# The first rows of a token mixer: statistics behind low parts, products by readiness, shorter scales

## The chip, the cores and the metric

The kernel runs on one core of a Trainium2 chip. The metric is device time in microseconds (us) of that core, the median of several runs. The engines work at the same time and wait for each other on semaphores: TensorE (PE in the profile) for matrix products, VectorE (DVE), ScalarE (ACT), GpSimd (POOL), and SyncE (SP), which here only issues loads and stores. Each engine works through its own queue in order.

## What is computed

```python
xn = layernorm(x)                                    # x: (1, 2048, 512), over the last axis
s  = irfft2(rfft2(xn) * (w_r + 1j * w_i))            # spectral branch
u  = gelu(einsum("bsd,sf->bdf", layernorm(xn), w1) + b1)   # w1: (2048, 1792)
y  = einsum("bdf,fs->bds", u, w2) + b2               # w2: (1792, 2048)
out = x + s * silu(y.transpose(0, 2, 1))
```

The layer norm is applied twice in the token branch and once in the spectral branch, so every token needs two factors: `rs[0]` and `rs[1]`, one over the root of `v2[0]` = var + eps and of `v2[1]` = var (1 + eps) + eps squared. The token branch uses `rs[1]` alone; the spectral branch takes the product `q` of `rs[0]`, `rs[1]` and `v2[1]`.

## The kernel before

Tokens are split into 16 rows of 128 partitions x 512 channels. Every operand of the big products is split into a high part (rounded) and a low part (the rest), and a product is made as high x high, high x low and low x high. In the first stage, 16 turns `j` of a loop accumulate six blocks of the hidden layer (two halves `a` of three blocks, `NE1`), in banks 0 to 5. This stage starts while the loads still run; the change touches its first rows. Later stages (the other hidden blocks, the spectral filter, the second weight product) are not touched.

**One row.** For row `j`, VectorE takes the statistics of x (`stats`, `bn_stats`), `spreads` turns them into mean and variance and into `v2`, ScalarE takes the square root (`sd`), and `scales` makes the factors on VectorE: the reciprocal `r0`, one Newton step (`t` = `r0`², `t` times -0.5 times `v2`, `rs` = (1.5 + `t`) times `r0`), then `nb`, minus mean times `rs[1]`; GpSimd multiplies `q`. ScalarE makes `h` from x by `nb` and `rs[1]` (`normed`, two halves) and its high part `hh` by a rounding copy (`high`), VectorE the low part `hl` (`low`). The weights of the row come as two raw tiles, `raws[j, 0]` and `raws[j, 1]`; ScalarE rounds each to its high part (`w1h`) and VectorE makes its low part (`w1l`), which the trace calls `w1l<-w1r,w1h`. `turned` makes the row's factor table `cf` from `q` on ScalarE, for the small transform of the spectral branch, which every second turn puts between the products.

**Row 0** is made differently: VectorE writes `hh[0]` straight from x (`normed_v`), between the factors and `nb`.

**Products.** `hidden_early` gives per half `a`: three products high x high, three with the low weights, then (after the transform where there is one) three with the low h. That makes six groups of three per row.

**Order.** All these instructions are kept in the order of the program on each engine (`keep`), so the order of the code is the order of each engine's queue. Turn 0 is special (`early` is false): it also takes the statistics of rows 2 and 3, before the low parts of row 1. From turn 1 on, turn `j` takes the statistics of row `j + 3` before the low parts of row `j + 1`; at even turns `spreads` and `scales` handle two rows at a time.

**Loads.** x comes in pairs of rows (`load_x`, three buffers), weights in pairs of rows (`w1_load`, two buffers per half), each as two DMAs. For row 0, row 1's x and weights, the DMAs are issued one by one by SP, ScalarE and GpSimd (`issued`). A load into a used buffer waits until its readers are done.

Before the first row, TensorE multiplies zeros (tile `wz`) 18 times.

Of the kernel before, what the change touches and what calls it, by code (L numbers as in the profile page):

```python
# [16 lines left out]
P = 128  # L17
# [125 lines left out]
def spectral_mixer_kernel(tc, x, w1, b1, w2, b2, wk, we, wx, c_f, c_ft, c_d, c_i, c_g, c_h, c_t, out):  # L143
# [19 lines left out]
    with tc.tile_pool(name="ps", bufs=1, space=PSUM) as psp, ExitStack() as left, ExitStack() as right:  # L163
# [54 lines left out]

        def stats(m, i, src):
            keep(V.bn_stats(m["st"][:, i], src))  # L220
# [12 lines left out]
        def scales(m, between=lambda: None):  # L233
# [6 lines left out]

            G.tensor_mul(m["q"], m["rs"][:, :, 0:1], m["rs"][:, :, 1:2])
            G.tensor_mul(m["q"], m["q"], m["v2"][:, :, 1:2])
# [206 lines left out]

        def hidden_early(j, nf, bank, w, between):  # L450
            def products(wi, hj, first, last):
                for i in range(nf):
                    T.matmul(ps[:, bank + i], w[wi][:, i * P:(i + 1) * P], hj, start=first and j == 0, stop=last and j == NJ - 1)
            products(0, hh[j], True, False)
            products(1, hh[j], False, False)
            r = between()
            products(0, hl[j], False, True)
            return r

        stats(m, 0, xs[0])  # L460
        spreads(m, 1)
# [3 lines left out]
        scales(m, lambda: normed_v(hh[0], xs[0], m, 0, 1))  # L465
# [4 lines left out]
        high(w[1][0], raws[0, 1])  # L470
        spreads(m1, 1)
        low(hl[0], h, hh[0])
        scales(m1)
        low(w[1][1], raws[0, 1], w[1][0])
        of = {0: (m, 0), 1: (m1, 0)}
# [8 lines left out]
        for j in range(NJ):  # L484
# [16 lines left out]
            hidden_early(j, NE1, 0, w[0], first_transform if j % 2 or j == NJ - 2 else lambda: None)  # L501
            hidden_early(j, NE1, NE1, w[1], lambda: None)

            early = j > 0
            if more:
                w = w1_tiles(j + 1)
                h = new_h(j + 1)
                if not early:
                    high(w[0][0], raws[j + 1, 0])
                normed(h, xs[j + 1], *of[j + 1])  # L510
                high(hh[j + 1], h)
                if early and j + 3 < NJ:
                    stats(of[j + 3][0], of[j + 3][1], xs[j + 3])
                    if j % 2 == 0:
                        spreads(of[j + 2][0], 2)
# [5 lines left out]
            if more:  # L521
                if early and j % 2 == 0 and j + 2 < NJ:
                    scales(of[j + 2][0])
                if not early:
# [3 lines left out]
                low(w[0][1], raws[j + 1, 0], w[0][0])  # L528
                high(w[1][0], raws[j + 1, 1])
                low(hl[j + 1], h, hh[j + 1])  # L530
                for i in range(j + early, j + 2):
                    turns[i] = turned(i, *of[i])
            run(folds)
            if more:
# [6 lines left out]
                if not early:  # L541
                    scales(m)
                if j % 2 == 0 and j + 4 < NJ:
# [560 lines left out]
```

## Time and profile before

| | us |
|---|---|
| median of 3 runs | 369.25 |
| lowest, highest | 368.75, 369.63 |
| profiled execution | 369.14 |
| its span | 367.4 |
| TensorE busy | 359.8 |
| VectorE busy | 305.2 |
| ScalarE busy | 210.5 |
| GpSimd busy | 85.0 |

The span runs from the first to the last instruction of the profiled execution; the remaining 1.74 us of its time lie around it. Line numbers (L448) are those of the kernel before. A helper of one line records many operations: most products stand at L140. In the rows, `h` stands for a row's tile whether as `h`, high or low part; three 128x512 products make one group. `PE` rows of a timeline are merged: their end is modelled, their start is not.

### The profile page before, as it was taken

What the parts mean: (1) busy time and instruction counts of PE and PEld (TensorE: products, weight loads), DVE (VectorE), ACT (ScalarE), POOL (GpSimd) and SP (SyncE); (2) the same over time, 40 slices, a digit from 0 to 9 for tenths busy, and PEclk for the clock granted to TensorE, in tenths of its full rate; (3) what the DMA queues carried; (4) which work ended last, traced back from release to release, by engine and by line L of the source; (5) the groups of instructions that cost most, each with busy time, mean ns of one, the idle gap of its engine ahead of it and who ended that gap; (6) DMA issues with size and microseconds to landing.
All of it is one profiled execution on the core that took longest, in us unless ns stands there. A gap on an engine that the chain in (4) does not pass through costs nothing.

```text
span 367.4 us, 8767 instructions
## 1 busy us (share of the span) xinstructions
PE 359.8 (98%) x3442; PEld 308.3 (84%) x3442; DVE 305.2 (83%) x586; ACT 210.5 (57%) x381; POOL 85.0 (23%) x126
## 2 busy tenths in 40 slices
PE   7999999999999999999999999999999999999994
PEld 4778888778777787777888999989898989898983
DVE  5799999984799997999994978787787969696983
ACT  4697887648734425765435875645564546565541
POOL 3133332332221022210120001050413223140330
PEclk9999999999999999999999999999999999999999
DMA  7977997704796677896567287698888989897724
GB/s 209 241 176 171 238 291 221 249 2 116 179 253 196 220 228 189 237 241 218 169 220 175 100 205 173 183 191 198 187 188 208 168 234 159 240 147 215 126 31 85
DMA packets 33449, 68.66 MB, mean 187 GB/s; under 512 B 4768, under 2 KB 19536, under 8 KB 33280
## 3 DMA queue, kind: packets, MB, share of 16 engines
q1 hardware_dynamic: 24432, 42.44, 41.8%
q0 software_dynamic: 8496, 25.01, 32.4%
q10 hardware_dynamic: 480, 0.66, 0.6%
q8 instruction: 27, 0.44, 0.5%
q14 instruction: 14, 0.11, 0.1%
HBM read 59.70 MB, written 8.13 MB: 185 GB/s over the span
## 4 chain that ended last, share of the span: by engine, by line
PE 92%; DMA 3%; DVE 2%; SPq 1%; issue 0%; ACTq 0%; ACT 0%; DVEq 0%
PE ps L140 92%; DMA x<-in_x_dram 2%; DMA w1r<-in_w_dram 1%; SPq L198 1%; DVE w1l L448 0%; DVE rows L140 0%; DVE stm L220 0%; DVE h L448 0%; ACTq L431 0%; DVE tm L235 0%; ACT g L140 0%; SPq L431 0%; DVE ey L287 0%; DVE t L284 0%; DVE t L283 0%
## 5 line engine op out<-in xcount | busy, mean ns | idle before, releaser
L140 PE MATMUL ps<-h,w1h 128*128 128x512 f32 x400 | 116.5, 398 | 0.7 <-DVE nbm L239 0.7
L140 PEld LDWEIGHTS ps<-h,w1h 128*128 128x128 f32 x400 | 72.8, 188 | 20.6 <-issue 4.9
L140 PE MATMUL ps<-h,w1l 128*128 128x512 f32 x200 | 68.1, 393 | 0.7 <-DVE w1l L448 0.6
L140 DVE TENSOR_TENSOR w2f<-a,w2f 128x896 fp32r<-128x896 f32 x36 | 39.2, 1089 | 22.1 <-ACT w2f L140 22.1
L140 PEld LDWEIGHTS ps<-h,w1l 128*128 128x128 f32 x200 | 37.2, 188 | 10.2 <-DVE w1l L448 2.3
L140 ACT ACTIVATE w2f<-a 128x896 fp32r<-128x896 f32 x36 | 36.8, 1023 | 12.6 <-PE ps L140 8.0
L140 PE MATMUL ps<-fb,w2f 128*128 128x256 f32 x336 | 41.9, 279 | 0.0
L140 PE MATMUL ps<-fa,w2f 128*128 128x256 f32 x336 | 41.3, 278 | 0.0
L140 PEld LDWEIGHTS ps<-fb,w2f 128*128 128x128 f32 x336 | 39.7, 188 | 1.7 <-ACT g L140 0.8
L140 POOL DMA_DIRECT2D s<-in_w_dram x14 | 18.2, 1300 | 98.9 <-DMA s<-in_w_dram 50.2
L140 PE MATMUL ps<-fc,w2f 128*128 128x256 f32 x336 | 39.9, 277 | 0.0
L140 PEld LDWEIGHTS ps<-fa,w2f 128*128 128x128 f32 x336 | 39.8, 188 | 0.0
L140 PEld LDWEIGHTS ps<-fc,w2f 128*128 128x128 f32 x336 | 39.2, 188 | 0.0
L140 POOL DMA_DIRECT2D out_dram<-r x28 | 23.7, 1287 | 27.1 <-DVE r L140 27.1
L156 ACT ACTIVATE w1h<-w1s 128x512 fp32r<-128x512 f32 x26 | 16.2, 632 | 20.6 <-PE ps L140 12.7
L630 POOL DMA_DIRECT2D xc<-xc x16 | 9.8, 618 | 70.1 <-ACT xc L628 55.1
L286 POOL TENSOR_TENSOR ey<-t 128x256 f32<-128x256 f32 x16 | 15.7, 980 | 43.8 <-DVE t L284 43.8
L140 ACT ACTIVATE w2f<-s 128x896 fp32r<-128x896 f32 x15 | 15.3, 1022 | 13.6 <-PE ps L140 12.5
L448 DVE TENSOR_TENSOR w1l<-w1r,w1h 128x384 fp32r<-128x384 f32 x32 | 21.3, 666 | 0.1
L140 PE MATMUL ps<-fd,w2f 128*128 128x256 f32 x168 | 20.6, 277 | 0.0
L140 ACT ACTIVATE g<-c,b2t 128x256 f32<-128x256 f32 x24 | 12.1, 505 | 14.6 <-DVE c L140 14.6
L140 PEld LDWEIGHTS ps<-fd,w2f 128*128 128x128 f32 x168 | 20.0, 188 | 0.1
(118 smaller groups left out, 598.2 us busy)
## 6 DMA issues: line engine op xcount, KB each, us to landing
a<-in_w_dram SPq DMA_DIRECT2D x22, 448.0 KB, 4.9
wt<-in_wk_dram POOLq DMA_DIRECT2D x16, 512.0 KB, 5.7
s<-in_w_dram SPq DMA_DIRECT2D x16, 448.0 KB, 5.0
s<-in_w_dram POOLq DMA_DIRECT2D x16, 448.0 KB, 6.9
w1s<-in_w_dram SPq DMA_DIRECT2D x52, 128.0 KB, 5.6
w1r<-in_w_dram SPq DMA_DIRECT2D x28, 192.0 KB, 5.9
xc<-xc POOLq DMA_DIRECT2D x16, 256.0 KB, 3.0
out_dram<-in_x_dram SPq DMA_DIRECT2D x4, 960.0 KB, 6.6
```

The source lines that it names most:

```text
L140: return lambda *args, **kw: self.keep(operation(*args, **kw))
L156: return A.activation(hi, src, AF.Copy), V.tensor_sub(lo, src, hi.bitcast(F32))
L198: last = SY.dma_start(to[64 * e:64 * e + 64], src[e::2])
L286: G.tensor_add(ey[:, 0::3, :, j], a, b)
L448: keep(V.tensor_sub(dst, src, hi.bitcast(F32)))
L630: keep(G.dma_start(*(v.rearrange("p s t c -> p s (t c)") for v in (there[c::2], here[1 - c::2, ::-1]))))
```

## The change

Three things are moved or rewritten, all in the first rows.

**Scales of rows 0 and 1.** `first_roots` and `first_scales` take the place of `spreads` and `scales` for these two rows. `t` is now `v2` times -0.5, made right behind `v2`, and `refined` multiplies `r0` by `r0` by `t` and then makes `rs`, for one of the two factors at a time. Only `rs[1]` is made at once; `rs[0]` of both rows follows later, behind the low part of row 0's second weights, and with it GpSimd's products.

**Row 0's products.** The groups of three come as: both halves high x high, low weights of half 0, both halves with the low h, low weights of half 1. ScalarE rounds `raws[0, 1]` before it makes `h` of row 0. Row 1's high part is made from x a second time by `normed`, ahead of `h`, in place of the rounding copy.

**Statistics.** Those of rows 2 and 3 come behind the low part of row 1's first weights. That of row 4 moves from before row 2's low parts to behind them. The factor tables of rows 0 and 1 move ahead of the rounding of row 1's second weights.

```diff
--- before.py
+++ after.py
@@ -216,6 +216,29 @@
                     for k, w in (("st", 6), ("mv", 2), ("v2", 2), ("sd", 2), ("r0", 2), ("t", 2), ("rs", 2), ("nb", 1),
                                  ("q", 1))}
 
+        def first_roots(m):
+            var = m["mv"][:, 0, 1:2]
+            keep(V.bn_aggr(m["mv"][:, 0], m["st"][:, 0]))
+            keep(V.tensor_scalar(m["v2"][:, 0, 1:2], var, 1.0 + EPS, EPS * EPS, op0=ALU.mult, op1=ALU.add))
+            keep(V.tensor_scalar(m["v2"][:, 0, 0:1], var, EPS, None, op0=ALU.add))
+            keep(A.activation(m["sd"], m["v2"], AF.Sqrt))
+            keep(V.tensor_scalar(m["t"], m["v2"], -0.5, None, op0=ALU.mult))
+
+        def refined(m, k):
+            t, r0, rs = (m[n][:, 0, k:k + 1] for n in ("t", "r0", "rs"))
+            keep(V.scalar_tensor_tensor(t, r0, r0, t, op0=ALU.mult, op1=ALU.mult))
+            keep(V.scalar_tensor_tensor(rs, t, 1.5, r0, op0=ALU.add, op1=ALU.mult))
+
+        def first_scales(m, between=lambda: None):
+            keep(V.reciprocal(m["r0"], m["sd"]))
+            refined(m, 1)
+            between()
+            keep(V.scalar_tensor_tensor(m["nb"], m["mv"][:, :, 0:1], -1.0, m["rs"][:, :, 1:2], op0=ALU.mult, op1=ALU.mult))
+
+        def product_of_scales(m):
+            G.tensor_mul(m["q"], m["rs"][:, :, 0:1], m["rs"][:, :, 1:2])
+            G.tensor_mul(m["q"], m["q"], m["v2"][:, :, 1:2])
+
         def stats(m, i, src):
             keep(V.bn_stats(m["st"][:, i], src))
 
@@ -237,9 +260,7 @@
             keep(V.scalar_tensor_tensor(m["rs"], m["t"], 1.5, m["r0"], op0=ALU.add, op1=ALU.mult))
             between()
             keep(V.scalar_tensor_tensor(m["nb"], m["mv"][:, :, 0:1], -1.0, m["rs"][:, :, 1:2], op0=ALU.mult, op1=ALU.mult))
-
-            G.tensor_mul(m["q"], m["rs"][:, :, 0:1], m["rs"][:, :, 1:2])
-            G.tensor_mul(m["q"], m["q"], m["v2"][:, :, 1:2])
+            product_of_scales(m)
 
         def normed(dst, src, m, i):
             for to, v in zip(mirrored(dst, False), mirrored(src, True)):
@@ -447,31 +468,35 @@
         def low(dst, src, hi):
             keep(V.tensor_sub(dst, src, hi.bitcast(F32)))
 
+        def products_early(j, nf, bank, wi, hj, first, last):
+            for i in range(nf):
+                T.matmul(ps[:, bank + i], wi[:, i * P:(i + 1) * P], hj, start=first and j == 0, stop=last and j == NJ - 1)
+
         def hidden_early(j, nf, bank, w, between):
-            def products(wi, hj, first, last):
-                for i in range(nf):
-                    T.matmul(ps[:, bank + i], w[wi][:, i * P:(i + 1) * P], hj, start=first and j == 0, stop=last and j == NJ - 1)
-            products(0, hh[j], True, False)
-            products(1, hh[j], False, False)
+            products_early(j, nf, bank, w[0], hh[j], True, False)
+            products_early(j, nf, bank, w[1], hh[j], False, False)
             r = between()
-            products(0, hl[j], False, True)
+            products_early(j, nf, bank, w[0], hl[j], False, True)
             return r
 
         stats(m, 0, xs[0])
-        spreads(m, 1)
+        first_roots(m)
         w = w1_tiles(0)
         h = new_h(0)
         high(w[0][0], raws[0, 0])
-        scales(m, lambda: normed_v(hh[0], xs[0], m, 0, 1))
+        first_scales(m, lambda: normed_v(hh[0], xs[0], m, 0, 1))
+        high(w[1][0], raws[0, 1])
         normed(h, xs[0], m, 0)
         m1 = moments("m1", 1)
         stats(m1, 0, xs[1])
         low(w[0][1], raws[0, 0], w[0][0])
-        high(w[1][0], raws[0, 1])
-        spreads(m1, 1)
+        first_roots(m1)
         low(hl[0], h, hh[0])
-        scales(m1)
+        first_scales(m1)
         low(w[1][1], raws[0, 1], w[1][0])
+        for i in (m, m1):
+            refined(i, 0)
+            product_of_scales(i)
         of = {0: (m, 0), 1: (m1, 0)}
         m = moments("m2", 2)
         of.update({2: (m, 0), 3: (m, 1)})
@@ -498,8 +523,12 @@
                 SY.dma_start(out[q, :NJ - 1], x[q, :NJ - 1])
 
             normal.append((j, h))
-            hidden_early(j, NE1, 0, w[0], first_transform if j % 2 or j == NJ - 2 else lambda: None)
-            hidden_early(j, NE1, NE1, w[1], lambda: None)
+            if j:
+                hidden_early(j, NE1, 0, w[0], first_transform if j % 2 or j == NJ - 2 else lambda: None)
+                hidden_early(j, NE1, NE1, w[1], lambda: None)
+            else:
+                for k, (a, n, hj) in enumerate(((0, 0, hh), (1, 0, hh), (0, 1, hh), (0, 0, hl), (1, 0, hl), (1, 1, hh))):
+                    products_early(j, NE1, NE1 * a, w[a][n], hj[0], k < 2, False)
 
             early = j > 0
             if more:
@@ -507,9 +536,11 @@
                 h = new_h(j + 1)
                 if not early:
                     high(w[0][0], raws[j + 1, 0])
+                    normed(hh[j + 1], xs[j + 1], *of[j + 1])
                 normed(h, xs[j + 1], *of[j + 1])
-                high(hh[j + 1], h)
-                if early and j + 3 < NJ:
+                if early:
+                    high(hh[j + 1], h)
+                if j > 1 and j + 3 < NJ:
                     stats(of[j + 3][0], of[j + 3][1], xs[j + 3])
                     if j % 2 == 0:
                         spreads(of[j + 2][0], 2)
@@ -521,15 +552,18 @@
             if more:
                 if early and j % 2 == 0 and j + 2 < NJ:
                     scales(of[j + 2][0])
+                low(w[0][1], raws[j + 1, 0], w[0][0])
+                if not early:
+                    for i in range(2):
+                        turns[i] = turned(i, *of[i])
+                high(w[1][0], raws[j + 1, 1])
                 if not early:
                     for i in range(2):
                         stats(m, i, xs[2 + i])
                     spreads(m, 2)
-                low(w[0][1], raws[j + 1, 0], w[0][0])
-                high(w[1][0], raws[j + 1, 1])
                 low(hl[j + 1], h, hh[j + 1])
-                for i in range(j + early, j + 2):
-                    turns[i] = turned(i, *of[i])
+                if early:
+                    turns[j + 1] = turned(j + 1, *of[j + 1])
             run(folds)
             if more:
                 low(w[1][1], raws[j + 1, 1], w[1][0])
@@ -540,6 +574,8 @@
                     low(w1_early[i][:, 1], pairs[i // 2][:, i % 2], w1_early[i][:, 0])
                 if not early:
                     scales(m)
+                if j == 1:
+                    stats(of[4][0], of[4][1], xs[4])
                 if j % 2 == 0 and j + 4 < NJ:
                     m = moments(f"m{j + 4}", 2)
                     of.update({j + 4: (m, 0), j + 5: (m, 1)})
```

VectorE from the low part of row 0's second weights (`w1l1_0`) to the low parts of row 1, before (`m2` belongs to the statistics of rows 2 and 3; `w1l0_1` is the low part of row 1's first weights):

```order
L448 TENSOR_TENSOR w1l1_0_165<-w1r1_0_103,w1h1_0_164 128x384
L220 BN_STATS stm2_204<-x1_123 128x6 x2
L230 BN_AGGR mvm2_205<-stm2_204 128x2 x2
L224 TENSOR_SCALAR v2m2_206<-mvm2_205 128x2
L225 TENSOR_SCALAR v2m2_206<-mvm2_205 128x2
L448 TENSOR_TENSOR w1l0_1_232<-w1r0_0_102,w1h0_1_231 128x384
L448 TENSOR_TENSOR h1_84<-h1_235,h1_84 128x512
L448 TENSOR_TENSOR w1l1_1_234<-w1r1_0_103,w1h1_1_233 128x384
```

The same place with the change:

```order
L469 TENSOR_TENSOR w1l1_0_166<-w1r1_0_103,w1h1_0_165 128x384
L229 SCALAR_TENSOR_TENSOR tm0_118<-r0m0_117,tm0_118 128x1
L230 SCALAR_TENSOR_TENSOR rsm0_119<-tm0_118,r0m0_117 128x1
L229 SCALAR_TENSOR_TENSOR tm1_183<-r0m1_182,tm1_183 128x1
L230 SCALAR_TENSOR_TENSOR rsm1_184<-tm1_183,r0m1_182 128x1
L469 TENSOR_TENSOR w1l0_1_236<-w1r0_0_102,w1h0_1_235 128x384
L243 BN_STATS stm2_208<-x1_123 128x6 x2
L253 BN_AGGR mvm2_209<-stm2_208 128x2 x2
L247 TENSOR_SCALAR v2m2_210<-mvm2_209 128x2
L248 TENSOR_SCALAR v2m2_210<-mvm2_209 128x2
L469 TENSOR_TENSOR h1_84<-h1_239,h1_84 128x512
L469 TENSOR_TENSOR w1l1_1_238<-w1r1_0_103,w1h1_1_237 128x384
```

Four small instructions and `w1l0_1` now stand ahead of the two `BN_STATS` of rows 2 and 3.

VectorE from `nb` of rows 2 and 3 to `v2` of rows 4 and 5, before:

```order
L239 SCALAR_TENSOR_TENSOR nbm2_211<-mvm2_205,rsm2_210 128x2
L220 BN_STATS stm4_262<-x2_136 128x6
L448 TENSOR_TENSOR w1l0_2_331<-w1r0_1_130,w1h0_2_330 128x384
L448 TENSOR_TENSOR h2_85<-h2_334,h2_85 128x512
L448 TENSOR_TENSOR w1l1_2_333<-w1r1_1_131,w1h1_2_332 128x384
L220 BN_STATS stm4_262<-x2_136 128x6
L230 BN_AGGR mvm4_263<-stm4_262 128x2 x2
L224 TENSOR_SCALAR v2m4_264<-mvm4_263 128x2
L225 TENSOR_SCALAR v2m4_264<-mvm4_263 128x2
```

The same place with the change:

```order
L262 SCALAR_TENSOR_TENSOR nbm2_215<-mvm2_209,rsm2_214 128x2
L469 TENSOR_TENSOR w1l0_2_336<-w1r0_1_130,w1h0_2_335 128x384
L469 TENSOR_TENSOR h2_85<-h2_339,h2_85 128x512
L469 TENSOR_TENSOR w1l1_2_338<-w1r1_1_131,w1h1_2_337 128x384
L243 BN_STATS stm4_267<-x2_136 128x6 x2
L253 BN_AGGR mvm4_268<-stm4_267 128x2 x2
L247 TENSOR_SCALAR v2m4_269<-mvm4_268 128x2
L248 TENSOR_SCALAR v2m4_269<-mvm4_268 128x2
```

The first `BN_STATS` of `stm4` (row 4) moved from ahead of row 2's three low parts to behind them.

ScalarE from row 0's weights to the factor tables of rows 0 and 1, before (`w1h1_0` is the high part of row 0's second weights):

```order
L445 ACTIVATE w1h0_0_162<-w1r0_0_102 128x384
L246 ACTIVATE h0_166<-x0_101,nbm0_120,rsm0_119 128x2x128 x2
L445 ACTIVATE w1h1_0_164<-w1r1_0_103 128x384
L226 ACTIVATE sdm1_182<-v2m1_181 128x2
L445 ACTIVATE w1h0_1_231<-w1r0_0_102 128x384
L246 ACTIVATE h1_235<-x0_101,nbm1_186,rsm1_185 128x2x128 x2
L445 ACTIVATE h1_84<-h1_235 128x512
L226 ACTIVATE sdm2_207<-v2m2_206 128x4
L445 ACTIVATE w1h1_1_233<-w1r1_0_103 128x384
L258 ACTIVATE cf0_250<-cf_62,qm0_121 128x64
L258 ACTIVATE cf1_252<-cf_62,qm1_187 128x64
```

The same place with the change:

```order
L466 ACTIVATE w1h0_0_163<-w1r0_0_102 128x384
L466 ACTIVATE w1h1_0_165<-w1r1_0_103 128x384
L267 ACTIVATE h0_167<-x0_101,nbm0_120,rsm0_119 128x2x128 x2
L224 ACTIVATE sdm1_181<-v2m1_180 128x2
L466 ACTIVATE w1h0_1_235<-w1r0_0_102 128x384
L267 ACTIVATE h1_84<-x0_101,nbm1_185,rsm1_184 128x2x128 x2
L267 ACTIVATE h1_239<-x0_101,nbm1_185,rsm1_184 128x2x128 x2
L279 ACTIVATE cf0_246<-cf_62,qm0_121 128x64
L279 ACTIVATE cf1_248<-cf_62,qm1_186 128x64
L466 ACTIVATE w1h1_1_237<-w1r1_0_103 128x384
L249 ACTIVATE sdm2_211<-v2m2_210 128x4
```

`w1h1_0` moved ahead of `h0`, the rounding copy into `h1` became a second pair from x, and the tables `cf` moved ahead of `w1h1_1` and of the root of rows 2 and 3.

## Rows read from the trace of the kernel before

**Rows 1.** The page, busy time by engine, and the chain that ended last

```profile
PE 359.8 (98%) x3442; PEld 308.3 (84%) x3442; DVE 305.2 (83%) x586; ACT 210.5 (57%) x381; POOL 85.0 (23%) x126
...
PE 92%; DMA 3%; DVE 2%; SPq 1%; issue 0%; ACTq 0%; ACT 0%; DVEq 0%
```

**Rows 2.** Stretches: length, busy us by engine, granted TensorE clock, DMA share, GB/s

```profile
14.20:23.20 9.00, 8.88 (x98) 7.13 (x97) 6.75 (x25) 7.15 (x16) 1.89 (x4) 1.00 0.91 210
...
92.00:362.40 270.40, 270.36 (x2589) 238.20 (x2587) 227.96 (x378) 144.69 (x243) 56.90 (x77) 1.00 0.77 187
362.40:367.40 5.00, 0.00 (x0) 0.00 (x0) 0.91 (x3) 0.47 (x1) 0.00 (x0) 1.00 0.39 105
```

**Rows 3.** Timeline of TensorE, rows 0 to 3: start, us, operation, [idle before <-releaser]

```profile
7.13 0.93 PE L140 MATMUL ps<-h,w1h 128*128 128x512 f32 x3 [0.75 <-DVE nbm L239]
...
13.29 0.98 PE L140 MATMUL ps<-h,w1l 128*128 128x512 f32 x3 [0.45 <-DVE w1l L448]
...
17.47 1.53 PE L140 MATMUL ps<-h,w1h 128*128 128x512 f32 x6
...
20.88 0.84 PE L140 MATMUL ps<-h,w1l 128*128 128x512 f32 x3
...
21.56 1.52 PE L140 MATMUL ps<-h,w1h 128*128 128x512 f32 x6
...
23.26 0.96 PE L140 MATMUL ps<-h,w1l 128*128 128x512 f32 x3 [0.18 <-DVE w1l L448]
```

**Rows 4.** The chain of work in order of time: start, us, what

```profile
9.49 7.49 DMA x<-in_x_dram
...
23.26 36.84 PE ps L140 x394
```

**Rows 5.** Timeline of VectorE from row 0's low part to row 3's

```profile
8.38 0.68 DVE L448 TENSOR_TENSOR h<-h,h 128x512 fp32r<-128x512 f32 x1
...
9.55 0.16 DVE L237 SCALAR_TENSOR_TENSOR rsm<-tm,r0m 128x2 f32<-128x2 f32 x1
9.75 0.16 DVE L239 SCALAR_TENSOR_TENSOR nbm<-mvm,rsm 128x1 f32<-128x1 f32 x1
9.83 0.57 DVE L448 TENSOR_TENSOR w1l<-w1r,w1h 128x384 fp32r<-128x384 f32 x1
11.00 1.29 DVE L220 BATCH_NORM_STATS2 stm<-x 128x6 f32<-128x512 f32 x2 [0.60 <-DMA x<-in_x_dram]
...
12.68 0.55 DVE L448 TENSOR_TENSOR w1l<-w1r,w1h 128x384 fp32r<-128x384 f32 x1
...
15.02 0.16 DVE L239 SCALAR_TENSOR_TENSOR nbm<-mvm,rsm 128x2 f32<-128x2 f32 x1
17.01 0.69 DVE L220 BATCH_NORM_STATS2 stm<-x 128x6 f32<-128x512 f32 x1 [1.83 <-DMA x<-in_x_dram]
...
21.63 0.50 DVE L235 TENSOR_TENSOR tm<-r0m 128x4 f32<-128x4 f32 x1
...
22.64 0.56 DVE L448 TENSOR_TENSOR w1l<-w1r,w1h 128x384 fp32r<-128x384 f32 x1
```

**Rows 6.** Row 0's second weights: an issue, and time to landing (last column)

```profile
2.91 0.62 ACTq L431 DMA_DIRECT2D w1r<-in_w_dram  x1
...
w1r<-in_w_dram SPq DMA_DIRECT2D x1, 96.0 KB, 3.9
```

**Rows 7.** Timeline of ScalarE: h of row 0, weights of rows 0 and 2

```profile
7.09 1.09 ACT L246 ACTIVATE h<-x,nbm,rsm 128x256 f32<-128x256 f32 x2 [0.86 <-DVE nbm L239]
...
8.09 0.51 ACT L445 ACTIVATE w1h<-w1r 128x384 fp32r<-128x384 f32 x1
...
16.87 0.92 ACT L445 ACTIVATE w1h<-w1r 128x384 fp32r<-128x384 f32 x2
```

**Rows 8.** Timeline of GpSimd: row factors, and the fold's sum

```profile
9.94 0.65 POOL L242 TENSOR_TENSOR qm<-qm,v2m 128x1 f32<-128x1 f32 x2
...
21.13 0.98 POOL L286 TENSOR_TENSOR ey<-t 128x256 f32<-128x256 f32 x1 [5.61 <-DVE t L284]
```

## The prediction

> **What bounds the kernel now.** I read the page's busy shares and chain first: the last chain of work is 92% TensorE, and TensorE is busy 98% of the span [rows 1]. Next comes the table of stretches, to see where the other 2% lie: from 92 to 362.4 us TensorE is busy 270.36 of 270.40 us, while between 14.2 and 23.2 us it still loses 0.12 us [rows 2], and the timeline of TensorE shows its waits in the ramp: 0.75 us before the first real product at 7.13, 0.45 us before row 1's low part at 13.29, 0.18 us before row 3's low part at 23.26 [rows 3]. These are the visible gaps; starts tell more. Three products take 0.68 us in steady work (20.88 to 21.56), 0.227 us each, so the six at 21.56 are over at 22.92 and the product at 23.26 starts 0.34 us late. The list of the chain shows that it runs from 23.26 on through TensorE alone, and that what lies before is not TensorE: a load of x that ends 16.98 (9.49 + 7.49) [rows 4].
>
> So the rule for this change: **only what moves the start at 23.26 moves the end.** From there TensorE never waits. Before it, everything that TensorE gains is slack if the product at 23.26 (row 3's first weight low part, written by VectorE 22.64 to 23.20 [rows 5]) does not come earlier. I therefore follow VectorE's chain to that instruction, not TensorE's.
>
> In the kernel before, VectorE idles 0.60 us until 11.00 for rows 2 and 3 of x, and 1.83 us until 17.01 for rows 4 and 5 [rows 5]. From 17.01 to 22.64 it works through statistics of row 4, the three low parts of row 2, statistics of row 5, the fold and the scales: 5.63 us, with one instruction (row 4's and 5's squares, 21.63) stretched to 0.50 us [rows 5].
>
> **The change, part by part.** *Shorter chain of scales for row 0.* The multiplication by -0.5 runs in the pause in which VectorE waits for the square root, and one link of the chain is gone. A link is 0.20 us (9.55 to 9.75 [rows 5]), so the first product starts at about 6.93 instead of 7.13 [rows 3]. That is a gain on TensorE alone, by the rule above worth nothing by itself.
>
> *Row 0's second weights rounded ahead of row 0's h on ScalarE.* Half of their load was issued at 2.91 by ScalarE; the other half, issued by SP in the same stretch, took 3.9 us to land, so an estimate of the landing is 6.8 [rows 6]. The rounding takes 0.51 us with some 0.1 of it overlapped, so h of row 0 starts at 7.2 instead of 7.09 and ends at 8.3 [rows 7]. VectorE reaches the low part of h only at 8.38 [rows 5], also with the one multiplication more in front. Cost: nothing, covered by VectorE's own queue, with 0.1 us to spare.
>
> *Row 1's scales.* One link less: nb of row 1 at 9.55 instead of 9.75, weight low part at 9.63 instead of 9.83, done at 10.2 [rows 5].
>
> *Four small instructions for the row factors, and the low part of row 1 ahead of the statistics.* The four now stand on VectorE behind that low part: two links of 0.20 and two steps of 0.08 (9.75 to 9.83), 0.56 us. They start at 10.12, and row 1's low part starts at 10.68 instead of 12.68. It holds VectorE 0.47 us (12.68 to the next, 0.55 with 0.08 overlapped, as the two statistics of 0.69 that take 1.29 show), so the statistics of rows 2 and 3 start at 11.15 instead of 11.00. The x that ended the wait at 11.00 has landed by then, so the 0.60 us of waiting are filled with work. From that start to nb of rows 2 and 3 it was 11.00 to 15.02, 4.02 us; without the 0.47 that moved ahead 3.55. So nb comes at 14.70, **0.32 us earlier** than 15.02.
>
> *ScalarE behind it.* h, its rounding and the weights of row 2 follow nb (15.02) without a pause: the pair of weight roundings starts at 16.87, the first is done 0.51 later, at 17.38 [rows 7]. 0.32 us earlier gives 17.06. The second reading of x for row 1 takes the place of a rounding copy, and the factors' copies stand in front of row 1's second weights; 9.55 and 0.2, twice 1.09, two small copies and 0.51 end near 12.8, when the square root of rows 2 and 3 comes due. Hidden.
>
> *TensorE.* With the products of row 0 in order of readiness it finds its operands: 6.93 plus 36 products of 0.227 and a transform of 1.46 us (13.29 to 17.47 less 12 products) puts the end of row 1 near 16.6. Row 2's first product was at 18.16 (the first three of the six at 17.47 [rows 3]); now it waits for the weights of 17.06 and starts at 17.1. TensorE is 1.05 us ahead here.
>
> *Statistics of rows 4 and 5 behind the low parts of row 2.* VectorE no longer waits for the x of 16.98. It now waits for the weights of row 2, 17.06 plus 0.04 of signalling: it restarts at 17.10, where before it restarted at 17.01. Behind the restart stand the same instructions as before, only in another order, up to row 3's low part: 5.63 us again. 17.10 + 5.63 = 22.73 against 22.64. So the product at 23.26 comes at **23.35, 0.09 us later**, and the 1.05 us of TensorE turn into one wait of about 1.4 us (17.1 plus 21 products of 0.227, row 2's 18 and row 3's first three, is 21.9). What is late next is therefore what was late before; a DMA wait has become a wait on the ScalarE chain that ends within 0.1 us of it.
>
> Bounds. From below: if the four small instructions hid completely, statistics would start at 11.00 at the earliest, when the x is there: 0.15 us better, -0.06 in all. From above: GpSimd now multiplies row 0's and 1's factors just as VectorE takes the moved low part. Where both ran in the trace before, one GpSimd pair took 0.65 us (9.94) and the squares at 21.63 ended with GpSimd's sum (21.13 + 0.98 = 22.11) after 0.50 us [rows 5, 8]. One such block costs up to 0.34 us (0.50 less a usual 0.16), so +0.43 in all. I take +0.09, since the moved low part is nearest to the one at 9.83, which took 0.57 with GpSimd at work beside it.
>
> [...]
>
> Everything behind 23.3 keeps its order, so it moves by the same amount. Loads: the fourth load of x waits for the second reading of row 1's x, some 0.8 us longer; its statistics stand behind row 3's low parts, after 23.3, so nobody waits for it.
>
> **The sum.** Profiled execution: 369.14 us, span 367.4 and 1.74 around it; 369.14 + 0.09 = 369.2. The median of the three runs, 369.25, is 0.11 above it, so 369.3 on that scale.
>
> **Rivals.** *A, the lead survives.* TensorE keeps its 1.05 us: 369.25 - 1.05 = 368.2. For it: the waits at 7.13 and 13.29 are real and go. Against it: row 3's low part must then come at 21.7, and of VectorE's 5.63 us only the 0.34 of the stretched squares is loose. It could still be partly so if the x of 16.98 lands later in most runs than in this one; only the kernel before would pay for that. Chance 0.10.
>
> *B, slower: the load in front of h.* Row 0's h now stands on ScalarE behind a rounding that waits for a load. VectorE works from 8.38 to nb of rows 2 and 3 with no pause, so each tenth by which that load lands after 6.9 goes straight to the end. [...] Chance 0.07.
>
> *C, the clock.* [...] Chance 0.03.
> [...]
>
> **How the numbers follow.** My case (nothing gained, -0.06 to +0.43) has 0.80; A 0.10, B 0.07, C 0.03. Its own range, with 0.4 us for the spread of the runs shown (368.75 to 369.63), is 368.8 to 370.0. The range reaches a little into A, to 368.4; to 370.0 above. Less than 0.2% (0.74 us) is about what a measurement can't tell from no change: faster 0.10, same 0.80, slower 0.10.
>
> **What would show it.** Right, if the changed profile has the first product near 6.9, no VectorE wait for x at 11 and 17, statistics of rows 2 and 3 near 11.1, nb of rows 2 and 3 near 14.7, a TensorE wait of about 0.5 us on ScalarE's weights near 17.1, and the longest TensorE wait, above 1 us, on VectorE's low part of row 3 ending near 23.3, with the chain on TensorE alone from there. Wrong, if that wait is short and ends before 22.6 (A), if VectorE idles before the low part of h at 8.4 (B), or if the granted clock leaves 1.00 (C).

## The result, and the profile after

The changed kernel takes **370.2 us** (median of 7 runs, 369.49 to 370.53) against 369.08 us (7 runs, 368.75 to 369.63) for the kernel before: a ratio of 1.0032, 95% interval 1.0019 to 1.0045. It is slower by about 1.1 us, where the prediction had no change and a range up to 370.0. A second comparison (below) gave 1.0036 (1.0023 to 1.0049).

The page of the changed kernel, as [rows 1]: VectorE has four instructions more, and the chain that ended last is TensorE for 79% only.

```profile
PE 359.0 (98%) x3442; PEld 307.8 (84%) x3442; DVE 306.1 (83%) x590; ACT 211.4 (57%) x382; POOL 84.8 (23%) x126
...
PE 79%; DVE 10%; DMA 5%; SPq 2%; issue 2%; ACT 1%; DVEq 0%; ACTq 0%
```

The chain in order of time (start, us, what), as [rows 4]: TensorE alone holds it from 71.87, not from 23.26.

```profile
71.87 290.85 PE ps L140 x2803
```

TensorE's timeline, as [rows 3]. Its waits at 13.29 and 23.26 have given way to two others: 0.44 us for ScalarE at 17.41 and 1.45 us for VectorE at 23.97, where the product that started at 23.26 now starts, 0.71 us later. One more wait, 0.16 us, stands at 71.87.

```profile
7.06 1.63 PE L140 MATMUL ps<-h,w1h 128*128 128x512 f32 x6 [0.53 <-DVE nbm L236]
...
17.41 0.97 PE L140 MATMUL ps<-h,w1h 128*128 128x512 f32 x3 [0.44 <-ACT w1h L466]
...
23.97 0.98 PE L140 MATMUL ps<-h,w1l 128*128 128x512 f32 x3 [1.45 <-DVE w1l L469]
...
71.87 0.98 PE L140 MATMUL ps<-h,w1l 128*128 128x512 f32 x3 [0.16 <-DVE w1l L469]
```

VectorE's timeline, as [rows 5]. No wait for x is left. But the bias (`nb`) of row 1 comes at 9.74 (9.75 before), the four small instructions (10.30 to 10.98) take 0.68 us, the bias of rows 2 and 3 comes at 15.00 (15.02), and the wait for ScalarE's weights ends at 17.39. At the fold (L304 to L308, three additions on the result of the small transform) stands a gap of 0.24 us that the kernel before doesn't have, and one of 0.20 us at 58.92.

```profile
9.29 0.22 DVE L229 SCALAR_TENSOR_TENSOR tm<-r0m,tm 128x1 f32<-128x1 f32 x1
...
9.74 0.16 DVE L236 SCALAR_TENSOR_TENSOR nbm<-mvm,rsm 128x1 f32<-128x1 f32 x1
...
10.30 0.21 DVE L229 SCALAR_TENSOR_TENSOR tm<-r0m,tm 128x1 f32<-128x1 f32 x1
...
10.98 0.56 DVE L469 TENSOR_TENSOR w1l<-w1r,w1h 128x384 fp32r<-128x384 f32 x1
11.46 1.28 DVE L243 BATCH_NORM_STATS2 stm<-x 128x6 f32<-128x512 f32 x2
...
15.00 0.16 DVE L262 SCALAR_TENSOR_TENSOR nbm<-mvm,rsm 128x2 f32<-128x2 f32 x1
17.39 0.56 DVE L469 TENSOR_TENSOR w1l<-w1r,w1h 128x384 fp32r<-128x384 f32 x1 [2.24 <-ACT w1h L466]
...
21.02 0.43 DVE L304 TENSOR_TENSOR t<-zt 128x256 f32<-128x256 f32 x1 [0.24 <-ACT sdm L249]
...
23.36 0.56 DVE L469 TENSOR_TENSOR w1l<-w1r,w1h 128x384 fp32r<-128x384 f32 x1
...
58.92 0.42 DVE L304 TENSOR_TENSOR t<-zt 128x256 f32<-128x256 f32 x1 [0.20 <-issue]
```

The releaser named at 21.02 is a coincidence: of ScalarE's work the instruction waits for its own copy alone, zt, done at 18.55. What the two additions share is their place: counted from 0 through the built program, semaphore instructions included, they are VectorE's instructions 64 and 192. In the kernel before, 64 and 192 are the squares of the scales (21.63 [rows 5]). They show no gap in front of them, and they take 0.50 us there as in the changed kernel, where they stand elsewhere.

So four theories went to the chip. **A**: the four instructions more cost 0.5 us in the chain, and their number moves two stalls of the instruction stream into view. **B**: the two gaps are waits for ScalarE or for rows that it holds late. **C**: the new order itself costs. **D**: the kernel before is better than its profile, since the wait for x that the change removes is one execution's landing.

### The profile page after: what moved, and what is told of

The parts are those of the page before. It is cut to its first block, busy times and chain, and to the rows that moved or that the text cites. A ratio compares the mean times of both kernels' runs of the same rounds, so it can differ in the third digit from the quotient of the medians.

```text
span 367.7 us, 8772 instructions
## 1 busy us (share of the span) xinstructions
PE 359.0 (98%) x3442; PEld 307.8 (84%) x3442; DVE 306.1 (83%) x590; ACT 211.4 (57%) x382; POOL 84.8 (23%) x126
## 4 chain that ended last, share of the span: by engine, by line
PE 79%; DVE 10%; DMA 5%; SPq 2%; issue 2%; ACT 1%; DVEq 0%; ACTq 0%
PE ps L140 79%; DMA w1e<-in_w_dram 2%; SPq L198 2%; DVE w1l L469 2%; DVE stm L243 2%; DMA out_dram<-in_x_dram 2%; DVE h L469 2%; DMA x<-in_x_dram 1%; DVE t L305 1%; DVE t L304 1%; DVE ey L308 1%; DVE tm L258 0%; DVE w1e L469 0%; ACT h L267 0%; DVE rows L140 0%
## 5 line engine op out<-in xcount | busy, mean ns | idle before, releaser
L267 ACT ACTIVATE h<-x,nbm,rsm 128x256 f32<-128x256 f32 (+1 forms) x34 | 18.4, 594 | 4.4 <-DVE nbm L262 4.0
```

The lines of the kernel that those rows point to most:

```text
L267: keep(A.activation(to, v, AF.Identity, bias=m["nb"][:, i], scale=m["rs"][:, i, 1:2]))
```

## Experiments

The runs are read by four numbers: VectorE's restart (what ended its long wait near 17, and when), the start of row 3's first low part, the start of TensorE's first product of 256 columns (where the later part of the program begins), and the span. "Wide" counts the stretches in which the products of 256 columns stand 118 ns apart instead of 113 (last section).

| kernel | restart, ended by | row 3's low part | first 256-column product | wide | span | ratio to before (95%) |
|---|---|---|---|---|---|---|
| before (profile ahead) | 17.01, load | 22.64 | 205.46 | 3 | 367.4 | 1 |
| before again | 16.56, load | 22.18 | 204.93 | 2 | 366.2 | 1.0000 (0.9989 to 1.0012) |
| after | 17.39, ScalarE | 23.36 | 206.47 | 2 | 367.7 | 1.0032 (1.0019 to 1.0045) |
| after again | 17.38, ScalarE | 23.35 | 206.45 | 3 | 368.4 | 1.0036 (1.0023 to 1.0049) |
| before, 4 idle instructions | 16.68, load | 22.66 | 205.72 | 3 | 367.6 | 1.0015 (1.0005 to 1.0025) |
| after, 12 idle instructions | 17.40, ScalarE | 23.03 | 205.82 | 3 | 367.7 | 1.0023 (1.0014 to 1.0032) |
| new order, old scales | 16.90, ScalarE | 22.54 | 205.31 | 3 | 367.2 | 1.0013 (1.0004 to 1.0022) |
| old order, new scales | 17.41, load | 23.38 | 206.46 | 2 | 367.7 | 1.0031 (1.0019 to 1.0044) |
| after, factors on GpSimd | 17.08, ScalarE | 22.72 | 205.52 | 2 | 366.8 | 1.0010 (0.9998 to 1.0021) |
| new order, row 4 first | 17.38, load | 23.02 | 205.86 | 2 | 367.1 | 0.9999 (0.9989 to 1.0010) |
| new order, weights early | 16.75, ScalarE | 21.92 | 204.93 | 3 | 366.8 | 0.9988 (0.9980 to 0.9997) |

Spans of single profiles differ by the landings and by "wide"; the ratios are over all runs of a comparison and need not be the quotient of two medians. In two rows, "before again" and "weights early", the first 256-column product is late for another reason, a slow start of TensorE (below). From the first product of 256 columns to the end it is 161.23 to 161.28 us with two wide stretches and 161.87 to 161.95 with three, in every row: the rest of the program is the same.

### Is it the place in the instruction stream?

```diff
+        pad = pers.tile([P, 1], F32, name="pad")
+        for _ in range(4):                      # 12 in the changed kernel
+            keep(V.memset(pad, 0.0))
         stats(m, 0, xs[0])
```

> The kernel before, with four one-column memsets put in front of VectorE's first statistics, where the engine is idle until 4.04 us. Nothing else moves. Theory A (place in the instruction stream): VectorE stalls at its instructions 64 and 192; four more instructions put the first addition of a fold there, as in the changed kernel. The fold's first addition at about 20.4 us then starts about 0.33 us later and so does the one at about 58.0 (0.29); row 3's first low part starts at about 22.97 instead of 22.64, and the time is about 0.6 us above the kernel before. Theory B (the two gaps of the changed kernel are waits for ScalarE or for rows that it holds late): idle instructions at the start change nothing, low part at 22.64, same time as before.

> The changed kernel, with twelve one-column memsets in front of VectorE's first statistics. Theory A: instruction 64 is now row 2's first low part, for which VectorE waits 2.2 us anyway, so the gap of 0.24 us in front of the fold at 21.02 goes and row 3's first low part starts at about 23.03 instead of 23.36; instruction 192 is now just ahead of row 10's first low part (about 54.6 us), so the second gap moves there from 58.92 and is not saved. Time about 0.3 us below the changed kernel. Theory B: both gaps stay where they are, and the time of the changed kernel stays.

Measured: 374.96 and 375.69 us, ratios 1.0175 and 1.0190. No theory had that. The gaps went as theory A says (in the kernel before one came at the fold, in the changed one it went), but the new tile lies among the persistent ones and moved the tiles behind it by 32 bytes, and the products of 256 columns became slower to the end. So the two were made again with a tile that is there already:

```diff
+        for _ in range(4):                      # 12 in the changed kernel
+            keep(V.memset(m["r0"], 0.0))
         stats(m, 0, xs[0])
```

> The kernel before, with four memsets of a tile that it has (r0 of row 0) in front of VectorE's first statistics: the run with four memsets of a new tile again, without the 32 bytes by which the new tile moved the tiles behind it. Theory A (place in the instruction stream): gaps of 0.2 us at the fold's first addition near 20 and near 58 us, each costing about 0.3 us, time about 0.6 us above the kernel before; no 6 us. Theory B: no gaps, the time of the kernel before.

> The changed kernel with twelve memsets of r0 of row 0 in front of VectorE's first statistics: the run with a new tile again, without the moved addresses. Theory A: no gap at the fold near 21 us, the second gap moved to about 54.6; time about 0.3 us below the changed kernel's, so 0.8 above the kernel before. Theory B: the changed kernel's time, 1.1 above before.

The kernel before with four idle instructions, VectorE: the gap is there, with the same wrong releaser, and from the restart to row 3's low part it takes 5.98 us, where "before again" takes 5.62.

```profile
16.68 0.69 DVE L220 BATCH_NORM_STATS2 stm<-x 128x6 f32<-128x512 f32 x1 [2.07 <-DMA x<-in_x_dram]
...
20.31 0.43 DVE L283 TENSOR_TENSOR t<-zt 128x256 f32<-128x256 f32 x1 [0.24 <-ACT sdm L226]
...
22.66 0.56 DVE L448 TENSOR_TENSOR w1l<-w1r,w1h 128x384 fp32r<-128x384 f32 x1
```

The changed kernel with twelve: same restart as without, no gap, and 5.63 us instead of 5.97.

```profile
17.40 0.56 DVE L469 TENSOR_TENSOR w1l<-w1r,w1h 128x384 fp32r<-128x384 f32 x1 [2.24 <-ACT w1h L466]
...
20.69 0.42 DVE L304 TENSOR_TENSOR t<-zt 128x256 f32<-128x256 f32 x1
...
23.03 0.56 DVE L469 TENSOR_TENSOR w1l<-w1r,w1h 128x384 fp32r<-128x384 f32 x1
```

Here the addition starts before the ScalarE instruction that the profile named as its releaser:

```profile
20.82 0.21 ACT L249 ACTIVATE sdm<-v2m 128x4 f32<-128x4 f32 x1 [0.64 <-DVE v2m L248]
```

So by the traces theory A holds for both stalls, and theory B falls. Each costs more than its gap, 0.34 and 0.3 us, as the overlap with the instruction before is lost too: without the stall the addition at 20.69 starts 0.09 us before the end of the instruction ahead of it (20.62 and 0.16 us). In the second kernel the second one is gone as well, against the expectation: instruction 192 is a semaphore instruction there; that the work around it covers the stall is not shown. Its first product of 256 columns starts at 205.82 instead of 206.47: 0.65 us for the two. The times are less sharp. The kernel with four is 0.6 us above before, as expected. The median of the one with twelve is 1.1 above before, where theory A had 0.8 and B 1.1 (0.5 to 1.2 by the interval): by its time alone B is not excluded, and that the two stalls' 0.65 us come back in the time is not shown. Its profile has one wide stretch more than the changed kernel's first, 0.63 us.

### Which part of the change?

New order, old scales (the functions `first_roots`, `first_scales` and `refined` give way to the old ones):

```diff
-        first_roots(m)
+        spreads(m, 1)
...
-        first_scales(m, lambda: normed_v(hh[0], xs[0], m, 0, 1))
+        scales(m, lambda: normed_v(hh[0], xs[0], m, 0, 1))
...
-        for i in (m, m1):
-            refined(i, 0)
-            product_of_scales(i)
```

> The order of the changed kernel (statistics of rows 2 and 3 behind the low part, row 0's products by readiness, row 1's h straight to high) with the old chain for the scales: no instruction more on VectorE than before. Theory A (the four instructions more delay the statistics, and move two stalls into view): statistics of rows 2 and 3 at about 10.9 us, their bias at 14.4, VectorE's restart at 16.8, no gap at the fold, row 3's first low part at 22.4; about 0.2 us below the kernel before, so 1.3 below the changed kernel. Rival C (the new order itself costs the time, the scales are neutral): row 3's first low part stays near 23.3 and the time near the changed kernel's.

Old order, new scales (the other half of the same diff, put into the kernel before):

> The kernel before with the changed kernel's chain for the scales alone, in the old order. Theory A: the four small instructions fall into the 0.60 us in which VectorE waits for row 2 of x, so the restart stays at 17.0; but instructions 64 and 192 are first additions of a fold again, and each costs about 0.3 us: row 3's first low part at about 23.0, time about 0.6 us above the kernel before. Rival C (the scales are neutral): low part at 22.6, same time as before.

The scales alone are slow by 1.0 us (1.0031), nearly as much as the whole change, where theory A had 0.6 (0.7 to 1.6 by the interval). Row 3's low part comes 5.97 us behind the restart, with the gaps of 0.25 and 0.21 us at the fold. The other 0.4 us are argued, not shown: the bias of rows 2 and 3 comes at 15.16, against 14.27 in "before again", so ScalarE has row 2's weights later and an early landing would be of less use. The order alone has no gap and its low part at 22.54, as theory A had it (22.4). Yet against medians it is 0.46 us slower, not 0.2 faster. Its own numbers were met; it was the kernel before that was better than its profile.

### How good is the kernel before?

> The kernel before, unchanged, as a kernel of its own: a second profile of it on another chip. Theory D (the 0.60 us that VectorE waited for row 2 of x at 11.00 is one execution's landing, not a property of the kernel): the rows land between 10.1 and 10.8 us here, the statistics of rows 2 and 3 start up to 0.55 us sooner, at 10.45 where the low part ends, and row 3's first low part starts between 21.9 and 22.6. Rival E (the landing is the same in every execution): statistics at 11.0 and low part at 22.64 as before. Time equal to that of the kernel before.

VectorE of the kernel before, on another chip: rows 2 and 3 of x are there when the low part ends (10.26), and rows 4 and 5 land 0.45 us sooner.

```profile
10.26 1.29 DVE L220 BATCH_NORM_STATS2 stm<-x 128x6 f32<-128x512 f32 x2
...
16.56 0.69 DVE L220 BATCH_NORM_STATS2 stm<-x 128x6 f32<-128x512 f32 x1 [2.12 <-DMA x<-in_x_dram]
...
22.18 0.56 DVE L448 TENSOR_TENSOR w1l<-w1r,w1h 128x384 fp32r<-128x384 f32 x1
```

In this execution TensorE waits for nothing after its first product, and the chain is its own from there:

```profile
7.05 354.14 PE ps L140 x3424
```

That TensorE meets every operand ready has a second cause, a slow start. Its first three products take 1.42 us (7.05 to 8.47), 0.47 each, against 0.23 in steady work (0.68 for three, as the prediction reads them):

```profile
7.05 1.62 PE L140 MATMUL ps<-h,w1h 128*128 128x512 f32 x3 [0.32 <-DVE nbm L239]
8.47 1.48 PE L140 MATMUL ps<-h,w1l 128*128 128x512 f32 x3
...
23.06 0.84 PE L140 MATMUL ps<-h,w1l 128*128 128x512 f32 x3
```

The profile's rows print a granted clock of 1.00 for this stretch, so the reason is not shown. Where this product waits, it starts 0.62 us behind its low part (22.64 and 23.26 ahead of the change, [rows 3, 5]). By that it could have started at 22.80, an estimate, and VectorE's chain is then the bound here too.

Theory D holds: the wait of 0.60 us at 11.00 [rows 5] is not a property of the kernel. Six executions, all with row 4's statistics in the old place, restart when rows 4 and 5 land, at 16.13 (the first run with four idle instructions), 16.56, 16.68, 17.01, 17.38 and 17.41. The changed kernel doesn't answer to the landing:

> The changed kernel again, for a second profile. Theory D (its start is bound by VectorE's chain and not by the landings): statistics of rows 2 and 3 at 11.4 to 11.5 us whatever the landing, gaps at the fold near 21.0 and 58.9, TensorE's wait for row 3's first low part 1.4 us, the first product of 256 columns at 206.3 to 206.5; about 1.1 us above the kernel before. If the landing sets it: that product moves by 0.5 us with the rows' landing, as in the kernel before.

Its rows 4 and 5 had landed at 15.75, a microsecond sooner than in the first profile (16.76), and yet it restarts at 17.38, has the gaps (0.25, 0.20) and reaches the first product of 256 columns at 206.45. The change has turned a restart at 16.1 to 17.4, when the load comes, into one at 17.4 in both of its profiles.

### The two costs undone

The new order, with the statistics of row 4 in front of row 2's low parts again:

```diff
-                if j > 1 and j + 3 < NJ:
+                if early and j + 3 < NJ:
                     stats(of[j + 3][0], of[j + 3][1], xs[j + 3])
...
-                if j == 1:
-                    stats(of[4][0], of[4][1], xs[4])
```

> The new order with the old scales, but the statistics of row 4 in front of row 2's low parts again, as in the kernel before. Theory D (that step costs when row 4 lands before ScalarE has row 2's weights, since VectorE idles there and has the work left over): VectorE takes row 4 while it waits for ScalarE, row 3's first low part comes at about 22.0 with an early landing and 22.6 with a late one, TensorE's wait for it is gone or under 0.2 us, and the first product of 256 columns is at 204.95 to 205.5 (205.31 in the new order); time that of the kernel before within 0.2 us, 0.4 below the new order. Rival C (the rest of the new order costs): the time stays 0.4 us above the kernel before.

The time is that of the kernel before, 368.6 us. Its profile fell on a late landing (VectorE restarts at 17.38 with row 4, low part at 23.02), later than the expectation allowed, and TensorE waits 0.64 us for it, where under 0.2 was expected. So only the time speaks: it is what this expectation's theory D had, and it points to the move of these statistics as the 0.4 us of the order. The intervals of the two runs (1.0004 to 1.0022, 0.9989 to 1.0010) still touch. The reason is argued: VectorE can take row 4 while it waits for ScalarE; behind the low parts the work, 0.6 us, is left over.

The changed kernel with the four small instructions on GpSimd:

```diff
-            refined(i, 0)
+            t, r0, rs = (i[n][:, 0, 0:1] for n in ("t", "r0", "rs"))
+            G.tensor_scalar(t, t, r0, r0, op0=ALU.mult, op1=ALU.mult)
+            G.tensor_scalar(rs, t, 1.5, r0, op0=ALU.add, op1=ALU.mult)
             product_of_scales(i)
...
-                if not early:
-                    for i in range(2):
-                        turns[i] = turned(i, *of[i])
...
                     spreads(m, 2)
+                    for i in range(2):
+                        turns[i] = turned(i, *of[i])
```

> The changed kernel with the four small instructions for the row factors of rows 0 and 1 on GpSimd instead of VectorE, and the two small products with them behind ScalarE's second rounding. VectorE has as many instructions as in the kernel before. Theory A (the four instructions cost their 0.5 to 0.7 us on VectorE, and by their number the two stalls): statistics of rows 2 and 3 at 10.8 us (11.46 with them), no gap at the fold near 20.3, row 3's first low part near 22.4, the first product of 256 columns at about 205.3 instead of 206.5; time about 0.7 us below the changed kernel's. [...]

368.94 us, against 370.19 for the changed kernel on the same chip: 1.25 us back, where 0.7 was expected. The first product of 256 columns starts at 205.52, 0.95 earlier, and no gap is left. The statistics started at 11.14, not at 10.8, mostly for a reason ahead of GpSimd's work: ScalarE waited for row 0's second weights until 7.23 (6.95 in the changed kernel), and the low part of h started at 8.78, not 8.50. GpSimd's instructions for the factors, 9.66 to 11.26 beside VectorE, came on top: the bias of row 1 took 0.21 us and came at 10.07 (0.16 us and 9.74 in the changed kernel).

### A version that beats both

```diff
+                if j == 1:
+                    high(w[0][0], raws[j + 1, 0])
                 normed(h, xs[j + 1], *of[j + 1])
...
-            if more and early:
+            if more and j > 1:
                 high(w[0][0], raws[j + 1, 0])
```

> The new order with the old scales, and ScalarE rounds row 2's first weights ahead of row 2's h, in its pause of 1.5 us before 14.7, so that VectorE makes their low part at 14.6 in place of waiting until 16.9. Theory F (from row 2 on the chain VectorE to ScalarE to VectorE sets the end): VectorE restarts with the low half of h at 16.4, row 3's first low part starts at 21.65 (22.54 without this), and the time falls by 0.9 us against the new order with old scales, to about 0.4 below the kernel before. Rival G (something else, a landing or ScalarE, is next in line): less than 0.3 us of it arrives.

368.17 us against 368.49, ratio 0.9988 (0.9980 to 0.9997). VectorE makes row 2's low part at 14.88 and restarts with h at 16.75, in an execution whose rows 4 and 5 landed at 17.36:

```profile
14.88 0.56 DVE L469 TENSOR_TENSOR w1l<-w1r,w1h 128x384 fp32r<-128x384 f32 x1
16.75 0.69 DVE L469 TENSOR_TENSOR h<-h,h 128x512 fp32r<-128x512 f32 x1 [1.32 <-ACT h L466]
...
21.92 0.56 DVE L469 TENSOR_TENSOR w1l<-w1r,w1h 128x384 fp32r<-128x384 f32 x1
```

Row 3's low part is 0.6 us earlier than in the order alone, of 0.9 expected; most of the rest is its later start, statistics of rows 2 and 3 at 11.22 instead of 10.96. TensorE shows no wait after its first product, and its first product of 256 columns comes at 204.93 with a late landing, as in "before again" with an early one. Both had a slow start: here the first nine products take 3.72 us, and the rows show the clock (stretch, length, busy us by engine, granted clock, DMA share, GB/s):

```profile
7.00:8.50 1.50, 1.37 (x4) 1.15 (x5) 1.42 (x6) 1.45 (x4) 0.00 (x0) 0.63 0.99 345
8.50:10.00 1.50, 1.50 (x5) 1.15 (x4) 1.27 (x6) 0.71 (x3) 0.00 (x0) 0.50 1.08 249
10.00:11.00 1.00, 1.00 (x4) 0.82 (x3) 1.00 (x3) 0.83 (x2) 0.98 (x3) 0.60 1.05 240
11.00:12.00 1.00, 1.00 (x6) 0.79 (x5) 0.87 (x3) 1.00 (x3) 0.14 (x1) 1.00 1.15 261
```

```profile
7.13 2.67 PE L140 MATMUL ps<-h,w1h 128*128 128x512 f32 x6 [1.63 <-DVE nbm L262]
9.59 1.42 PE L140 MATMUL ps<-h,w1l 128*128 128x512 f32 x3
10.85 1.55 PE L140 MATMUL ps<-h,w1h 128*128 128x512 f32 x6
...
23.08 0.84 PE L140 MATMUL ps<-h,w1l 128*128 128x512 f32 x3
```

TensorE had idled 1.63 us before 7.13. From 8.5 to 10 the granted clock is 0.50, and from 11 to 12 it is 1.00. So TensorE is the bound from its first product on in this execution, but not by the kernel alone: with the 0.62 us from above, row 3's product could have started at 22.54 instead of 23.08, an estimate. Whether this version gains more where TensorE starts at a granted clock of 1.00, no run shows.

## Why the prediction was wrong

**The step that failed** is the sum of VectorE's chain, "17.10 + 5.63 = 22.73 against 22.64", together with the step that all behind 23.3 moves by the same amount. It gave 0.09 us. The profile has 0.29 more for the restart (term 1), 0.34 more behind it (term 2) and 0.30 more behind 23.3 (term 3). With the 0.09 that is the 1.01 us (one hundredth is rounding) by which the first product of 256 columns comes later.

**The rule was right, the row it was tied to is not always the one.** What moved the end was indeed VectorE's chain to row 3's low part, and TensorE's lead turned into one wait (1.45 us, 1.4 predicted). That the size fits is luck: both of its ends came some 0.6 us later than predicted. But the chain's last piece doesn't always start at row 3: it starts at 23.x or at 71.87, by how late VectorE is and whether the second stall comes, and with the first product (7.05, 7.13) where TensorE starts slowly.

**Term 1, the restart: 17.10 predicted, 17.39 measured.** The links saved (0.20 for row 1) were eaten by what replaced them: the new form L229 takes 0.22 where 0.16 was assumed, and the added multiplication holds VectorE 0.08 us in front of the low part of h (8.50 instead of 8.42). The four small instructions took 0.68 instead of 0.56. Together the statistics start at 11.46, not 11.15, and all the rest of the chain, 3.54 us to the bias and 2.36 more to ScalarE's weights (3.55 and 2.36 predicted), was right. The 0.04 us of signalling in that sum were 0.02 here: ScalarE's rounding ended at 17.37 (16.85 and 0.52).

**Term 2, the same instructions and so 5.63 us again: 5.97 measured.** The instructions were the same, their places in VectorE's stream were not. This step failed by itself: 0.34 us, and neither bound had it. The block of up to 0.34 us taken for the upper bound didn't come, though GpSimd's pair ran beside the moved low part, which took 0.56 us (0.55 before):

```profile
10.86 0.73 POOL L239 TENSOR_TENSOR qm<-rsm 128x1 f32<-128x1 f32 x2 [5.03 <-DVE tm L229]
```

**Term 3, everything behind 23.3 moves by the same amount: 0.71 there, 1.01 at the first product of 256 columns.** The second stall, at 58.92, is the 0.3.

**Term 4, the side of before.** The 0.60 and 1.83 us of waiting for x were taken as cover for added work. That holds in the profiled execution. In "before again" the first wait is not there, and the second ends 0.45 us sooner. Of the rivals only A spoke of landings, and only of later ones. Taken from an early landing the sum is: 22.18, plus 0.36 (order: 22.54), plus 0.49 (new scales: 17.39 less 16.90), plus 0.33 (first stall), 23.36 as measured, and 0.3 for the second stall: some 1.5 us; from the late one 0.72 and 0.3, 1.0. The medians of the two comparisons are 1.1 and 1.55 us apart, by the ratios 1.2 and 1.3.

**Right:** no wait for x at 11 and 17, the wait for ScalarE near 17, the clock (rival C: in the changed kernel the granted clock is 1.00 through the wait of 1.45 us and behind it), row 0's second weights (rival B: the low part of h started at 8.50 without a wait, but with 0.04 us to spare, since h ended at 8.46 and not at 8.3; the run with the factors on GpSimd shows B's delay, 8.78). Small: the first product came at 7.06, not 6.93.

## What to carry to other kernels

A wait on a load in one profile can be that execution's landing: look at a second profile of the same kernel before work is put into the hole (the 0.60 us at 11.00 were not there in the second). Work that moves from "while we wait anyway" to "after the wait" can cost, even if its count stays the same: here the move of 0.6 us of statistics goes with ratios of 1.0013 and, undone, 0.9999, whose intervals touch. And when a change adds a few instructions to an engine that sets the end, compare the gaps of its stream before and after: here four instructions of 0.16 to 0.22 us cost as much again (0.68 us of their own, 0.65 for the two stalls, at the first product of 256 columns) by where the 64th and 192nd came to lie.

## What the hardware did that was not expected

**Stalls by position.** VectorE's gaps of 0.20 to 0.25 us stood in front of the fold's additions in the five profiles in which these were instructions 64 and 192, and in none of the others. Where another instruction stood there (the squares, or a low part that waited 2.24 us), no such gap shows. The two places are 128 apart, but the later places speak against a stall every 128: at 576, counted in the same way, the changed kernel has the third of four instructions that follow each other every 0.33 us, with no gap:

```profile
243.25 1.41 DVE L140 TENSOR_TENSOR r<-ps,g 128x256 f32<-128x256 f32 x4
```

The page lists two queues of the kind instruction, with 14 packets (0.11 MB) and 27 (0.44 MB); no view ties the stalls to them. So what is shown is the two stalls and their tie to the position; their cause is open.

**Two spacings of the same products.** From the first product of 256 columns on, groups of 21 start 2.48 or 2.38 us apart, 118 or 113 ns a product, at a granted clock of 1.00. The spacing is wide in the first two long stretches (15 and 17 us) of every profile at these addresses and in the third of some, narrow from then on, and doesn't change inside a stretch, apart from the first group of each, which takes 0.1 us more. The same products of the third stretch, in TensorE's timeline of the changed kernel's first profile and then of its second:

```profile
245.46 2.54 PE L140 MATMUL ps<-fd,w2f 128*128 128x256 f32 x21
247.84 2.54 PE L140 MATMUL ps<-fa,w2f 128*128 128x256 f32 x21
```

```profile
245.59 2.63 PE L140 MATMUL ps<-fd,w2f 128*128 128x256 f32 x21
248.07 2.63 PE L140 MATMUL ps<-fa,w2f 128*128 128x256 f32 x21
```

The third stretch is worth 0.63 us, over half of the change's effect, which is why the two first profiles differ by only 0.35 us. What selects the spacing in the third stretch is open.

It depends on where the tiles lie. The version that beats both was run again with 64 empty bytes in front of them:

> The new order with the old scales and row 2's weights rounded early, with 64 empty bytes among the persistent tiles, so that the tiles behind them lie 64 bytes further; no instruction changes. A new tile of one column moved them by 32 bytes, and the products of 256 columns came 118 to 121 ns apart to the end, at 6 us in all. Theory H (what counts is that moving columns and weights then differed in their address modulo 64): with 64 bytes the spacing stays at 113 ns, with 118 in two or three of the first stretches, and the time within 0.3 us of the same kernel without the space. Rival I (any move costs): some 6 us again.

372.81 us, ratio 1.0113: 4.6 us above the same kernel without the space, all of it behind the first product of 256 columns (204.90, unmoved, though this profile starts slowly too, 7.17 to 9.87 for its first six products). Theory H is refuted, since 64 bytes keep the address modulo 64, and the loss is of the order of that of 32 bytes (6 us): the two moves tried both cost. Which relation between the tiles of columns and weights matters was not tried.
